# Chunked attention with a gated feed-forward network on one core: tighter attention buffers and an earlier end of the weight sums

## The chip, the cores and the metric

The kernel runs on one core of a Trainium2 chip. The metric is the device time of one execution in microseconds; a kernel's time is the median of its runs. The kernel before takes 924.37 us (three runs, 924.31 to 925.99).

## The reference, cut to what matters

```
def _attn_ref(q, k, v):                      # (8, 8, 576, 64) each
    q_c = q.reshape(B, H, 9, 64, 64)         # and k_c, v_c: chunks of 64 tokens
    scores = scale * np.matmul(q_c, k_c.transpose(0, 1, 2, 4, 3))
    scores = scores - np.max(scores, axis=-1, keepdims=True)
    attn = np.exp(scores)
    attn = attn / (np.sum(attn, axis=-1, keepdims=True) + 1e-09)
    return np.matmul(attn, v_c)
...
    x = attn_out.transpose(0, 2, 1, 3).reshape(4608, 512)
    gate = 1.0 / (1.0 + np.exp(-(x @ w_gate)))       # 512 x 1536
    return gate * (x @ w_val) @ w_out                # 1536 x 512
```

Everything is fp32. The kernel writes a number as the sum of two parts that TensorE multiplies at its faster rate ("high", rounded, and "low", what is left) and makes three products of them, so one fp32 matmul is three instructions.

## The kernel before

The 4608 tokens are nine blocks of 512. Blocks 0 to 2 are computed directly, blocks 3 to 8 in three pairs by Strassen's scheme, with 7 products instead of 8 for each 2x2 block product.

**Direct blocks.** A step handles one of twelve groups of 128 hidden units for one block: `hidden` (L315) runs 24 matmuls of 512 columns for gate and value (L313), a sigmoid on ScalarE (L322), the product on VectorE (L324) and the split into high and low part `hx` (ScalarE L327, VectorE L328). `down` then runs 12 matmuls (L339) on the step before's hidden values. After the twelfth group `evacuate` copies the four finished tiles from PSUM, by VectorE (L357) and ScalarE (L355) in turn, into the two buffers of the tag "ob" (the last two tiles of block 2 into one of their own), from where they are stored.

**Attention** runs ahead of the blocks, as a generator `flow` in which each `yield` is a place to wait: `tick` gives it credit and lets it go on, `insert` places the matmuls. It goes by pairs of units (a unit is 256 tokens of four heads). For a pair: `products2` makes the scores (64 matmuls of 64x64, L192), VectorE takes off the maximum (L721, L722), ScalarE exponentiates (L726), VectorE sums, inverts, multiplies (L744 to L749) and transposes 32x32 blocks in place (L753); then 16 copies bring the blocks to their transposed places (`pbd`): all on ScalarE (L766) during blocks 1 and 2, half of them on GpSimd (L764) in the Strassen part (`joined`). `values2` multiplies with the values (64 matmuls, L207), and the result becomes the input block (`xt`, or `raw` for the Strassen part). Keys lie in `kbd` and transposed blocks in `pbd` with zeros beside each 64x64 block, since the first units (another routine) multiply blocks of twice the width; a unit's keys come with two loads. The scores after the maximum lie in one buffer `pr`.

**Weight sums.** The Strassen part needs sums and differences of weight blocks, which are made while blocks 1 and 2 run and put in DRAM. That is 36 items (`keep`, `keep_sums`): 24 of the sort stored in `sums`, 12 for the output weights, stored in `stream`. An item is two or three additions on VectorE (L400; L404 and L407) into a tile `a_val`, then five instructions on GpSimd: three additions (L409 to L411), a copy that makes the high part `a_high` (L413) and a subtraction that leaves the low part in `a_val` (L414). Two or four stores on SP's queue follow (L417; L421), high part first. `a_val` comes from the two buffers of "ob", which the block outputs use too. In `rest` 32 items are handed out evenly over the steps, 1.5 a step,

```
keep(min(32, 3 * (x + part) // 4))
```

so that the last falls in the step before the last of block 2; the four others (`late`, tile `a_late`, all on GpSimd) follow in groups 2, 4, 5 and 7 of the first Strassen pair.

**Operands.** Before the Strassen part starts, VectorE takes differences of the `raw` blocks (`differ` L461, `operands` L477), ScalarE makes high parts `xc` (L481) and VectorE low parts (L489). These stand among the last steps of block 2.

**Strassen part.** For each pair and each of twelve weight groups `first`, `middle` and `last` run 42 matmuls of products into `cx`, `cy`, `cz` (L499), with the sums that join them on VectorE, ScalarE and GpSimd (GpSimd: L527, L583, L584), and `outward` the output products (L640). `load_group` fetches the weights: L438 those that are given, L441 the sums.

The order on TensorE, VectorE and ScalarE is the order of the program (`manual_schedule`). On GpSimd and on SP, which issues all loads and stores, a scheduler sets it. An engine or queue takes its instructions in order, so one that waits holds all behind it.

## Time and profile before

| what | value |
|---|---|
| runs | 924.31, 924.37, 925.99 us |
| the profiled execution | 921.2 us |
| its span in the profile | 919.4 us |
| mean granted TensorE clock | 0.987 |
| TensorE busy | 891.3 us, 97% |
| VectorE, ScalarE, GpSimd busy | 607.5, 429.1, 268.3 us |

The profile is of one execution, whose own time is 921.2 us; the 1.8 us that it has over the span lie around the recorded instructions. Busy time counts instructions and not the waits of an engine. The granted clock is the share of TensorE's full speed. Times in the rows are microseconds from the start of the span. "[1.80 <-DVE ob L357]" means that the engine sat idle for 1.80 us before, until VectorE's instruction of line 357 that writes `ob` released it. PE is TensorE, DVE VectorE, ACT ScalarE, POOL GpSimd.

### The profile page before, as it was taken

Reading aid. Unit: us, or ns where it says so; the run is one execution under the profiler, and the core shown is the slowest. Engines: PE = TensorE matmul, PEld = TensorE weight load, DVE = VectorE, ACT = ScalarE, POOL = GpSimd, SP = SyncE. Lnnn points to the kernel's source line nnn. Section 1 sums busy time; section 2 is a strip of 40 time slices with the busy share of each in tenths; the row PEclk is TensorE's granted clock in tenths of the full one; section 3 lists DMA queues with packets and bytes.
Section 4 is the critical chain, followed back from the end, with each engine's and each line's share of the span. In section 5 each row is a group of like instructions: output and inputs, shape, how many; then the busy total and the mean of one; then the engine's idle time right before and its main releaser. Section 6 shows DMA issues by size and latency. Waiting matters only on the chain. (4 is left out here: it accounts for less than half of the span.)

```text
span 919.4 us, 15150 instructions
## 1 busy us (share of the span) xinstructions
PE 891.3 (97%) x5748; PEld 726.5 (79%) x5748; DVE 607.5 (66%) x894; ACT 429.1 (47%) x768; POOL 268.3 (29%) x325
## 2 busy tenths in 40 slices
PE   6999999999999998898999999999999999999998
PEld 4788879888877886687788888878788888888886
DVE  6999874656655559664666896566678953434884
ACT  5899753455544563254553642455336321112441
POOL 1000000556646658278352000353510002433000
PEclk8999999999999999999999999999999999999999
DMA  8698893344544485566984567775545686554553
GB/s 266 225 312 289 301 324 114 115 139 135 164 155 139 144 232 170 187 221 207 295 305 142 206 222 278 241 244 197 180 149 201 219 277 206 181 206 160 184 206 115
DMA packets 97464, 189.75 MB, mean 206 GB/s; under 512 B 8688, under 2 KB 56304, under 8 KB 93552
## 3 DMA queue, kind: packets, MB, share of 16 engines
q1 hardware_dynamic: 97392, 188.78, 61.6%
q8 instruction: 46, 0.75, 0.3%
q14 instruction: 26, 0.21, 0.1%
HBM read 146.28 MB, written 42.47 MB: 205 GB/s over the span
## 5 line engine op out<-in xcount | busy, mean ns | idle before, releaser
L313 PE MATMUL g<-xt,w 128*128 128x512 f32 (+1 forms) x960 | 210.5, 374 | 6.1 <-ACT hf L322 4.1
L313 PEld LDWEIGHTS g<-xt,w 128*128 128x128 f32 x960 | 168.8, 190 | 41.9 <-ACT hf L322 6.7
L640 PE MATMUL d<-hd,wd 128*128 128x512 f32 x756 | 172.4, 389 | 0.1
L640 PEld LDWEIGHTS d<-hd,wd 128*128 128x128 f32 x756 | 141.7, 188 | 30.3 <-DVE hd L620 0.9
L499 PE MATMUL cy<-xc,wr 128*128 128x512 f32 x648 | 159.8, 390 | 2.0 <-ACT ob L355 0.8
L499 PEld LDWEIGHTS cy<-xc,wr 128*128 128x128 f32 x648 | 121.4, 188 | 28.7 <-ACT ob L355 1.5
L499 PE MATMUL cx<-xc,wr 128*128 128x512 f32 x432 | 113.2, 398 | 2.6 <-DVE ob L357 2.6
L499 PE MATMUL cz<-xc,wr 128*128 128x512 f32 x432 | 111.1, 392 | 0.4 <-issue 0.3
L339 PE MATMUL acc<-w,hx 128*128 128x512 f32 x432 | 107.5, 396 | 2.4 <-DVE ob L357 1.8
L499 PEld LDWEIGHTS cx<-xc,wr 128*128 128x128 f32 x432 | 81.7, 191 | 20.5 <-DVE ob L357 3.1
L339 PEld LDWEIGHTS acc<-w,hx 128*128 128x128 f32 x432 | 80.2, 189 | 20.5 <-DVE ob L357 2.2
L499 PEld LDWEIGHTS cz<-xc,wr 128*128 128x128 f32 x432 | 80.3, 188 | 18.4 <-issue 1.6
L409 POOL TENSOR_TENSOR a_val<-a_val 128x128 f32<-128x128 f32 x32 | 16.9, 527 | 225.7 <-DVE a_val L400 212.8
L527 POOL TENSOR_TENSOR hid<-u,hid 128x512 f32<-128x512 f32 x15 | 19.3, 1290 | 205.4 <-DVE u L556 205.2
L515 ACT COPY s1u<-cx 128x512 f32<-128x512 f32 x36 | 21.2, 588 | 110.9 <-PE cx L499 107.4
L619 ACT CAST hd<-hid 128x1024 fp32r<-128x1024 f32 x48 | 49.9, 1051 | 49.2 <-PE d L640 37.3
L766 ACT COPY pbd<-pr 32x256 f32<-32x256 f32 x160 | 64.6, 403 | 5.8 <-DVE pr L753 3.7
L620 DVE TENSOR_TENSOR hd<-hid,hd 128x1024 fp32r<-128x1024 f32 x48 | 58.5, 1223 | 12.4 <-ACT hd L619 12.2
L324 DVE TENSOR_TENSOR hf<-g,hf 128x512 f32<-128x512 f32 (+1 forms) x40 | 25.3, 632 | 58.0 <-ACT hf L322 39.8
L764 POOL COPY pbd<-pr 32x256 f32<-32x256 f32 x64 | 25.3, 395 | 106.6 <-DVE pr L753 86.8
L517 DVE TENSOR_TENSOR s1u<-cy,s1u 128x512 f32<-128x512 f32 x36 | 24.8, 689 | 40.8 <-PE cy L499 40.7
L327 ACT CAST hx<-hf 128x512 fp32r<-128x512 f32 (+1 forms) x40 | 23.1, 578 | 60.9 <-DVE hf L324 60.9
(130 smaller groups left out, 1154.0 us busy)
## 6 DMA issues: line engine op xcount, KB each, us to landing
wr<-sums SPq DMA_DIRECT2D x72, 512.0 KB, 4.8
wd<-stream SPq DMA_DIRECT2D x30, 1024.0 KB, 4.6
w_raw<-w_in SPq DMA_DIRECT2D x36, 512.0 KB, 5.3
wr<-given SPq DMA_DIRECT2D x36, 512.0 KB, 3.8
qt<-q_in SPq DMA_DIRECT2D x36, 256.0 KB, 3.8
kbd<-k_in SPq DMA_DIRECT2D x72, 128.0 KB, 3.9
vt<-v_in SPq DMA_DIRECT2D x36, 256.0 KB, 3.8
given<-w SPq DMA_DIRECT2D x36, 256.0 KB, 4.8
```

The costliest lines, as they stand in the source:

```text
L313: nc.tensor.matmul(ps[:, tok], lhsT=wt[f, which][:, wpart, c:c + P], rhs=x[:, part, i, tok], start=n == 0, stop=n == 11)
L324: nc.vector.tensor_tensor(out=hf, in0=pv, in1=hf, op=ALU.mult)
L327: nc.scalar.copy(hh[:, tok], hf)
L339: nc.tensor.matmul(acc[m, t], lhsT=hx[:, ts], rhs=wt[f, 2][:, wpart], start=f == 0 and i == 0, stop=f == NF - 1 and i == 2,)
L499: nc.tensor.matmul(bank, lhsT=lhs(wpart, c), rhs=x[:, part, c], start=start and k == 0, stop=stop and k == 5, skip_group_check=True)
L515: nc.scalar.copy(s1, x)
L517: nc.vector.tensor_tensor(out=u2, in0=y, in1=s1, op=ALU.add)
L619: nc.scalar.copy(t[:, 0], at)
L620: nc.vector.tensor_tensor(out=t[:, 1], in0=at, in1=t[:, 0].bitcast(F32), op=ALU.subtract)
L640: nc.tensor.matmul(bank, lhsT=w[:, o:o + P], rhs=x[:, part], start=p == 0 and opening and i == 0, stop=p == 5 and i == 2, skip_group_check ...
L764: nc.gpsimd.tensor_copy(pb[dst, :, c, h, i, :], ps[src, h::2, k, :])
L766: nc.scalar.copy(pb[dst, :, c, h, i, :], ps[src, h::2, k, :])
```

## The change

- Keys and transposed blocks have no zeros from unit 8 on: a pair's keys are one tile `kt`, with one load a unit instead of two, its transposed blocks one tile `pt`. The four tiles of `kbd` and `pbd` go to a pool of their own with four places (k0, k1, p0, p1), which later tiles take over.
- The room is used twice: every second pair's `pr` lies in place k0 instead of the old buffer, and `a_val` becomes a tile for two items that alternates between place p1 and "spare", so four items are held instead of two. `a_high` takes the two buffers of "ob" instead.
- Sums are handed out at 1.8 a step instead of 1.5. The four late ones follow in groups 1, 3, 5 and 7.
- The 16 copies of a pair are half ScalarE's and half GpSimd's in blocks 1 and 2 too, in one piece. ScalarE's copies go from 160 to 112, GpSimd's from 64 to 112.
- The values' matmuls may be placed one tick sooner (`insert(upto, 1)`), the exponential waits for the next tick in blocks 1 and 2.

The numbers of instructions on TensorE and VectorE stay the same.

```diff
--- before.py
+++ after.py
@@ -70,9 +70,9 @@
     zeros = early[:, 0, 0].bitcast(mybir.dt.bfloat16)
     nc.vector.memset(zeros, 0.0)
 
-    kbd = [const.tile([P, 2, 2, 256], F32, name=f"kbd{i}") for i in range(2)]
-    pbd2 = const.tile([P, 2, 8, 2, D], F32, name="pbd")
-    pbd = [pbd2[:, i] for i in range(2)]
+    kp = ctx.enter_context(tc.tile_pool(name="kp", bufs=1))
+    kbd = [kp.tile([P, 2, 2, 256], F32, tag=f"k{i}", name=f"kbd{i}") for i in range(2)]
+    pbd = [kp.tile([P, 8, 2, D], F32, tag=f"p{i}", name=f"pbd{i}") for i in range(2)]
     for i in range(2):
         eng = nc.gpsimd if i else nc.vector
         eng.memset(kbd[i][0:D, :, 1, :], 0.0)
@@ -140,18 +140,24 @@
 
 
     units = [(m, h, u) for m in range(NB) for h in range(2) for u in range(2)]
-    state, both = {}, {}
+    state, both, keys, turned = {}, {}, {}, {}
     xt, raw = {}, {}
 
     def load(j):
         m, h, u = units[j]
         g = 2 * m + h
         qt = ap2.tile([P, 2, 256], F32, name="qt")
-        kb = kbd[j % 2]
         nc.sync.dma_start(qt, q[g, u].rearrange("p (a n) -> p a n", a=2))
-        for i in range(2):
-            s = slice(i * D, (i + 1) * D)
-            nc.sync.dma_start(kb[s, :, i, :], k[g, u, s].rearrange("p (a n) -> p a n", a=2))
+        if j < 8:
+            kb = kbd[j % 2]
+            for i in range(2):
+                s = slice(i * D, (i + 1) * D)
+                nc.sync.dma_start(kb[s, :, i, :], k[g, u, s].rearrange("p (a n) -> p a n", a=2))
+        else:
+            if j // 2 not in keys:
+                keys[j // 2] = kp.tile([P, 2, 2, 256], F32, tag="k1", name="kt")
+            kb = keys[j // 2][:, u]
+            nc.sync.dma_start(kb, k[g, u].rearrange("p (a n) -> p a n", a=2))
         state[j] = dict(qt=qt, kb=kb)
 
     def load_values(j):
@@ -192,14 +198,14 @@
                             nc.tensor.matmul(
                                 sc[i][c * D:(c + 1) * D, at:at + D],
                                 lhsT=s["qt"][i * D:(i + 1) * D, a, n0:n0 + D],
-                                rhs=s["kb"][i * D:(i + 1) * D, a, i, n0:n0 + D], start=True, stop=True)
+                                rhs=s["kb"][i * D:(i + 1) * D, a, n0:n0 + D], start=True, stop=True)
         return [x.rearrange("p (g k) -> p g k", k=D) for x in sc]
 
     def values2(j):
         av = [ps_a.tile([P, 512], F32, tag="psa", name="av") for _ in range(2)]
         for u in range(2):
             s = state.pop(j + u)
-            pb = pbd[(j + u) % 2]
+            pb = turned[j // 2][:, u]
             for c in range(4):
                 at = (4 * u + c) * D
                 for a in range(2):
@@ -207,7 +213,7 @@
                         nc.tensor.matmul(
                             av[i][a * D:(a + 1) * D, at:at + D],
                             lhsT=s["vt"][i * D:(i + 1) * D, a, c, :],
-                            rhs=pb[i * D:(i + 1) * D, 4 * a + c, i, :], start=True, stop=True)
+                            rhs=pb[i * D:(i + 1) * D, 4 * a + c], start=True, stop=True)
         m, h, _ = units[j]
         at = slice(h * 256, (h + 1) * 256)
         if m < FIRST_PAIR and h == 0:
@@ -365,7 +371,7 @@
 
 
 
-    given, sums, highs = {}, {}, {}
+    given, sums, vals = {}, {}, {}
     stream = dp.tile([P, 7, 6, 512], F32, name="stream")
 
     def keep_given(p, which):
@@ -389,8 +395,9 @@
             val, high = place_[:, 0, 0].bitcast(F32).rearrange("p (s n) -> p s n", n=P), place_[:, 1, 0]
         else:
             if c == 0:
-                highs[0] = wp.tile([P, 2, TB], F32R, tag="spare", name="a_high")
-            val, high = mp.tile([P, 4, P], F32, tag="ob", name="a_val"), highs[0][:, c]
+                pool, tag = ((wp, "spare"), (kp, "p1"))[(2 * p + which if which < 2 else p) % 2]
+                vals[0] = pool.tile([P, 2, 4, P], F32, tag=tag, name="a_val")
+            val, high = vals[0][:, c], mp.tile([P, TB], F32R, tag="ob", name="a_high")
         for n in range(2):
             eng = nc.gpsimd if late else nc.vector
             f = 2 * p + n
@@ -714,7 +721,10 @@
                     scv = products2(j, False)
                 if j + 2 < 4 * NB:
                     load(j + 2), load(j + 3)
-                pr = ap2.tile([P, 2, 8, D], F32, name="pr", bufs=1)
+                if j % 4 == 0:
+                    pr = ap2.tile([P, 2, 8, D], F32, name="pr", bufs=1)
+                else:
+                    pr = kp.tile([P, 2, 8, D], F32, tag="k0", name="pr")
                 for i in range(2):
                     yield 1.4
                     mx = sm.tile([P, 8], F32, name="mx")
@@ -753,17 +763,16 @@
                 nc.vector.transpose(out=half, in_=half)
             kept = True
             ps = pr.rearrange("p g (k j) -> p g k j", j=32)
-            pb = pbd2.rearrange("p u (x c) h (i q) -> p (u x) c h i q", c=2, q=32)
+            turned[j // 2] = kp.tile([P, 2, 8, D], F32, tag="p0", name="pt")
+            pb = turned[j // 2].rearrange("p u (x c) (i q) -> p (u x) c i q", c=2, q=32)
             for n in range(16):
-                if n == 0 or n == 8 and not now["joined"]:
+                if n == 0:
                     yield "piece"
                 c, i, h, k = n >> 3, n >> 2 & 1, n >> 1 & 1, n & 1
                 src = slice((2 * c + i) * 32, (2 * c + i + 1) * 32)
                 dst = slice((2 * h + k) * 32, (2 * h + k + 1) * 32)
-                if n % 2 and now["joined"]:
-                    nc.gpsimd.tensor_copy(pb[dst, :, c, h, i, :], ps[src, h::2, k, :])
-                else:
-                    nc.scalar.copy(pb[dst, :, c, h, i, :], ps[src, h::2, k, :])
+                eng = nc.gpsimd.tensor_copy if n % 2 else nc.scalar.copy
+                eng(pb[dst, :, c, i, :], ps[src, h::2, k, :])
 
     ahead = flow()
     now = dict(credit=0.0, ticks=0, since=0, unit=8, early=-1, open=-1, late=-1, up=-1, joined=False, place="")
@@ -785,6 +794,7 @@
                 now["credit"] -= now["item"]
             elif not (now["item"] == "piece" and now["ticks"] > now["since"] and now["place"] != "middle"
                       or now["item"] == "apart" and now["place"] != "middle"
+                      and now["ticks"] > now["since"] - now["joined"]
                       or now["item"] == "wait" and now["ticks"] > now["since"] + (not now["joined"])
                       or now["item"][0] in ("early", "open", "late", "up") and now["item"][1] <= now[now["item"][0]]):
                 break
@@ -861,8 +871,8 @@
                     if part:
                         finish()
                     tick(SHARES[m])
-                    insert(upto, 2)
-                    keep(min(32, 3 * (x + part) // 4))
+                    insert(upto, 1)
+                    keep(min(32, 9 * (x + part) // 10))
                 if m == 2:
                     if f == 8:
                         for which in range(2):
@@ -896,8 +906,8 @@
                     next(ending)
                 if i == 11:
                     now["open"] = n + 1
-                if n == 0 and i in (2, 4, 5, 7):
-                    keep(32 + (2, 4, 5, 7).index(i) + 1, True)
+                if n == 0 and i in (1, 3, 5, 7):
+                    keep(32 + i // 2 + 1, True)
                 if 0 < i < 11:
                     tick(SHARES["middle"], "middle")
             next(ending, None)
```

VectorE, end of block 2, where the Strassen operands are made (`raw`, `xc`; `a_val` are the sums). Before:

```order
L324 TENSOR_TENSOR hf<-g_3604,hf 128x512
L328 TENSOR_TENSOR hx<-hf,hx 128x512
L404 TENSOR_TENSOR a_val<-w 128x256
L407 TENSOR_TENSOR a_val<-w 128x128 x2
L461 TENSOR_TENSOR raw<-raw 128x2x512 x2
L489 TENSOR_TENSOR xc<-raw,xc 128x1024 x3
L324 TENSOR_TENSOR hf<-g_3716,hf 128x512
L328 TENSOR_TENSOR hx<-hf,hx 128x512
L477 TENSOR_TENSOR raw<-raw 128x2x512
L404 TENSOR_TENSOR a_val<-w 128x256
L407 TENSOR_TENSOR a_val<-w 128x128 x2
L489 TENSOR_TENSOR xc<-raw,xc 128x1024 x2
```

With the change:

```order
L330 TENSOR_TENSOR hf<-g_3635,hf 128x512
L334 TENSOR_TENSOR hx<-hf,hx 128x512
L468 TENSOR_TENSOR raw<-raw 128x2x512 x2
L496 TENSOR_TENSOR xc<-raw,xc 128x1024 x3
L484 TENSOR_TENSOR raw<-raw 128x2x512
L330 TENSOR_TENSOR hf<-g_3705,hf 128x512
L334 TENSOR_TENSOR hx<-hf,hx 128x512
L496 TENSOR_TENSOR xc<-raw,xc 128x1024 x2
L484 TENSOR_TENSOR raw<-raw 128x2x512 x2
L330 TENSOR_TENSOR hf<-g_3757,hf 128x512
```

The sums between the differences and the low parts are gone from there; the first row of both fences is the product of the step that makes the differences.

GpSimd, a pair in block 1 or 2: `a_val` and `a_high` are the sums. Before there are sums alone:

```order
L409 TENSOR_TENSOR a_val<-a_val 128x128
L410 TENSOR_TENSOR a_val<-a_val 128x128
L411 TENSOR_TENSOR a_val<-a_val 128x256
L409 TENSOR_TENSOR a_val<-a_val 128x128
L413 CAST a_high<-a_val 128x512
L410 TENSOR_TENSOR a_val<-a_val 128x128
L414 TENSOR_TENSOR a_val<-a_val,a_high 128x512
L411 TENSOR_TENSOR a_val<-a_val 128x256
L413 CAST a_high<-a_val 128x512
```

With the change a pair's eight copies (`pt<-pr`) come between them:

```order
L775 COPY pt<-pr 32x8x32 x4
L416 TENSOR_TENSOR a_val<-a_val 128x128
L775 COPY pt<-pr 32x8x32
L417 TENSOR_TENSOR a_val<-a_val 128x128
L775 COPY pt<-pr 32x8x32
L418 TENSOR_TENSOR a_val<-a_val 128x256
L775 COPY pt<-pr 32x8x32
L420 CAST a_high<-a_val 128x512
L775 COPY pt<-pr 32x8x32
L421 TENSOR_TENSOR a_val<-a_val,a_high 128x512
```

Four copies stand ahead of an item, the others alternate with its instructions.

GpSimd, first Strassen pair, ahead of the second group of copies. Before (the third late item, then a product of the hidden values and the copies):

```order
L404 TENSOR_TENSOR a_late<-w 128x256
L407 TENSOR_TENSOR a_late<-w 128x128 x2
L409 TENSOR_TENSOR a_late<-a_late 128x128
L410 TENSOR_TENSOR a_late<-a_late 128x128
L411 TENSOR_TENSOR a_late<-a_late 128x256
L413 CAST a_late<-a_late 128x512
L414 TENSOR_TENSOR a_late<-a_late 128x512
L527 TENSOR_TENSOR hid<-u_4224,hid 128x512
L764 COPY pbd<-pr 32x8x32 x8
```

With the change (the fourth late item):

```order
L411 TENSOR_TENSOR a_late<-w 128x256
L414 TENSOR_TENSOR a_late<-w 128x128 x2
L416 TENSOR_TENSOR a_late<-a_late 128x128
L417 TENSOR_TENSOR a_late<-a_late 128x128
L418 TENSOR_TENSOR a_late<-a_late 128x256
L420 CAST a_late<-a_late 128x512
L421 TENSOR_TENSOR a_late<-a_late 128x512
L534 TENSOR_TENSOR hid<-u_4226,hid 128x512
L775 COPY pt<-pr 32x8x32 x8
```

The rows have the same kinds and order; the late item is another one.

## Rows read from the trace of the kernel before

**Rows 1.** the page's part 1: engine, busy us (share of the span), instructions

```profile
PE 891.3 (97%) x5748; PEld 726.5 (79%) x5748; DVE 607.5 (66%) x894; ACT 429.1 (47%) x768; POOL 268.3 (29%) x325
```

**Rows 2.** windows: length, busy us of PE, PEld, DVE, ACT, POOL; clock, DMA share, GB/s

```profile
160.00:255.00 95.00, 95.00 (x828) 77.63 (x827) 56.19 (x93) 48.99 (x89) 57.16 (x75) 1.00 0.43 135
255.00:280.00 25.00, 22.57 (x150) 17.78 (x149) 13.18 (x21) 11.59 (x27) 11.08 (x15) 0.93 0.51 163
...
345.00:380.00 35.00, 27.94 (x105) 21.03 (x104) 26.29 (x29) 10.38 (x14) 22.34 (x17) 0.90 0.59 183
...
410.00:446.00 36.00, 32.85 (x310) 25.92 (x308) 19.79 (x31) 15.39 (x31) 28.62 (x40) 0.95 0.74 245
```

**Rows 3.** timeline of TensorE, a steady step: start us, duration us, operation, count

```profile
287.50 5.60 PE L313 MATMUL g<-xt,w 128*128 128x512 f32 x24
...
295.75 1.16 PE L192 MATMUL sc<-kbd,qt 64*64 64x64 f32 x64
```

**Rows 4.** timeline of TensorE, end of block 1; in brackets the idle time before

```profile
261.28 1.52 PE L339 MATMUL acc<-w,hx 128*128 128x512 f32 x6
...
268.80 5.74 PE L313 MATMUL g<-xt,w 128*128 128x512 f32 x24
...
277.88 5.73 PE L313 MATMUL g<-xt,w 128*128 128x512 f32 x24 [0.62 <-ACT hf L322]
```

**Rows 5.** timeline of VectorE, then of ScalarE, end of block 1

```profile
263.86 0.69 DVE L357 COPY ob<-acc 128x512 f32<-128x512 f32 x1 [5.50 <-DMA sums<-a_val]
...
270.58 6.63 ACT L766 COPY pbd<-pr 32x256 f32<-32x256 f32 x16
```

**Rows 6.** timeline of TensorE, end of block 2

```profile
347.52 2.88 PE L339 MATMUL acc<-w,hx 128*128 128x512 f32 x12
353.44 7.34 PE L313 MATMUL g<-xt,w 128*128 128x512 f32 x24 [3.04 <-ACT hf L322]
...
371.42 2.93 PE L499 MATMUL cx<-xc,wr 128*128 128x512 f32 x6 [2.65 <-DVE ob L357]
...
376.60 1.52 PE L499 MATMUL cx<-xc,wr 128*128 128x512 f32 x6
```

**Rows 7.** timeline of VectorE, of ScalarE and of GpSimd, end of block 2

```profile
345.46 1.52 DVE L404 TENSOR_TENSOR a_val<-w 128x256 f32<-128x256 f32 x1 [2.32 <-DMA stream<-a_val]
...
347.30 2.61 DVE L461 TENSOR_TENSOR raw<-raw 128x1024 f32<-128x1024 f32 x2
...
349.95 2.94 ACT L481 CAST xc<-raw 128x1024 fp32r<-128x1024 f32 x3 [5.81 <-DVE raw L461]
...
369.76 2.12 POOL L414 TENSOR_TENSOR a_val<-a_val,a_high 128x512 f32<-128x512 f32 x1
```

**Rows 8.** timeline of TensorE, first Strassen group

```profile
418.72 0.79 PE L207 MATMUL av<-pbd,vt 64*64 64x64 f32 x8 [1.24 <-POOL pbd L764]
...
443.39 1.63 PE L499 MATMUL cy<-xc,wr 128*128 128x512 f32 x6 [0.67 <-DMA wr<-sums]
```

**Rows 9.** timeline of GpSimd, then of SP's queue, first Strassen group

```profile
410.58 0.74 POOL L404 TENSOR_TENSOR a_late<-w 128x256 f32<-128x256 f32 x1 [4.01 <-DMA stream<-a_late]
...
417.41 3.49 POOL L764 COPY pbd<-pr 32x256 f32<-32x256 f32 x8
...
422.50 10.27 SPq L421 DMA_DIRECT2D stream<-a_late  x3
```

**Rows 10.** the tile a_val, GpSimd's instructions: count, duration ns min/median/max, first to last start

```profile
L409 POOL TENSOR_TENSOR a_val<-a_val x32: 450/460/1376, 166.8 to 365.1; 128x128 f32<-128x128 f32 x32
L410 POOL TENSOR_TENSOR a_val<-a_val x32: 453/462/1324, 167.3 to 365.7; 128x128 f32<-128x128 f32 x32
L411 POOL TENSOR_TENSOR a_val<-a_val x32: 725/738/1607, 167.9 to 366.5; 128x256 f32<-128x256 f32 x32
L413 POOL CAST a_high<-a_val x32: 604/611/1493, 168.7 to 368.2; 128x512 fp32r<-128x512 f32 x32
L414 POOL TENSOR_TENSOR a_val<-a_val,a_high x32: 1272/1291/2155, 169.4 to 369.8; 128x512 f32<-128x512 f32 x32
```

## The prediction, made before the run

> **What bounds the kernel now.** I read the page first: TensorE is busy for 891.3 of 919.4 us, the others far less [rows 1]. So time can only be won where TensorE waits, or where its clock was lowered after a wait. The windows say where that is [rows 2]. From 160 to 255 us TensorE is busy all the time at a granted clock of 1.00. It idles for 25.00 - 22.57 = 2.43 us between 255 and 280, for 7.06 us between 345 and 380 and for 3.15 us between 410 and 446, and there the clock is 0.93, 0.90 and 0.95. Counting a window's missing clock share as lost time too (25 x 0.07 + 35 x 0.10 + 36 x 0.05 = 7.1 us), some 19.7 us are lost in these three places. Whatever the change does elsewhere lies beside a TensorE that is full.
>
> The unit for the sums is a steady step: 36 matmuls of 512 columns take 295.75 - 287.50 = 8.25 us, so one takes 0.229 us, and a block of 64 small attention matmuls 1.16 us [rows 3].
>
> Loss A, the end of block 1: from 261.28 to 268.80 run 12 matmuls and one attention block in 7.52 us [rows 4]; 12 x 0.229 + 1.16 = 3.91 would do, so 3.6 are lost, and 0.62 more at 277.88. The other engines tell why [rows 5]: the output copy of VectorE at 263.86 had waited 5.50 us for a store of weight sums (same two buffers "ob"), and the later wait is for a sigmoid behind 16 block copies of ScalarE, 6.63 us long. Loss B, the end of block 2: from 347.52 to 376.60 run 12+24+12+6+12+6+6 = 78 matmuls in 29.08 us; 78 x 0.229 = 17.9, so 11.2 are lost [rows 6]. There VectorE's weight sum at 345.46 waits 2.32 us for its buffer's store, so the differences behind it come late, ScalarE's casts at 349.95 have waited 5.81 us for these, the sigmoid is queued behind the casts, and TensorE waits 3.04 us for the sigmoid. The wait of 2.65 us at 371.42 is for an output copy on the same full VectorE, which still interleaves weight sums; GpSimd's last sum ran at 369.76 [rows 7]. Loss C, the first Strassen group: values matmuls wait 1.24 us for GpSimd's copies at 417.41, queued behind a late sum that waited 4.01 us for a store at 410.58; and 0.67 at 443.39 is for weights whose load came late: SP's queue had stood for 10.27 us from 422.50 at a late sum's stores [rows 8, 9].
>
> **The change part by part.** *Early sums.* Now 32 items at 1.8 a step need 32/1.8 = 17.8 steps instead of 21.3, and the order shows none left in the last four steps of block 2, where before five were interleaved with the differences and lower halves. So the VectorE wait of 2.32 us, the sums between the differences and the GpSimd work of loss B go, and with them its waits and the half clock after them. Is something else late next? In the first of those steps VectorE has two differences (2.61 us for the two while it shared the time with sums [rows 7]) and then lower halves; it can run over a step of 8.25 us by a little and has three lighter steps to recover, and TensorE needs the hidden values only a step later. I take all of it: **-11.2**. Bounds: nothing (a new chain as long as the old) to 11.2.
>
> *Sums in four-deep buffers apart from "ob".* The output copies no longer share buffers with the sums' low part. They share them with the high part now, which is made and stored ahead of the low one. Of A's 3.6 + 0.6 = 4.2 us I take **-3.7**: ScalarE's 16 copies become 8, so the sigmoid comes about 3.3 us sooner and the 0.62 goes whole; of the 3.6 I leave 0.5 for a wait on the new neighbour. Bounds: 0.6 to 4.2.
>
> *GpSimd.* It has to do more in less time. An item is five instructions. Between 160 and 255 us 75 took 57.16 us, so 57.16 / 15 = 3.81 an item [rows 2]; the medians make 3.56, the slowest of each 7.96 [rows 10]. Per step: 1.8 x 3.81 = 6.86, and for each of six pairs eight copies of 3.49 us together [rows 9], 6 x 3.49 / 17.8 = 1.18; 8.04 in all. A step is 8.25 plus twelve attention blocks over 17.8 steps, 12 x 1.16 / 17.8 = 0.78, that is 9.03. GpSimd is 89% full: it keeps up, and I cost it **0** while its cover, the 1.0 us left a step, holds. It falls behind from an item of (9.03 - 1.18) / 1.8 = 4.36 us on.
>
> *Keys, transposed blocks, values a tick sooner.* One key load instead of two (28 issues fewer on SP), nothing removed on TensorE: **0** where TensorE is full. The values matmuls stand at least a group of 36 matmuls (8.25 us) behind their copies; GpSimd's half takes 3.49 us, with one item of 3.81 mixed in 7.30. Cover left: 1.0 us.
>
> *Late sums.* In the new orders all four stand ahead of the copies of 417.41, and the last stores ahead of the loads in question, so the wait at 443.39 goes: **-0.9** (0.67, and some lower clock; at least 0). The wait at 418.72 stays: where the third late item stood before the copies, the fourth now does, and it still needs an earlier item's store; with fewer loads on SP that store may come a little sooner. I take **-0.5**, between -4.3 (the window's 3.15 + 1.8, less 0.67) and, with an item's medians of 3.56 more in front of the copies, +3.6.
>
> Sum: 11.2 + 3.7 + 0.9 + 0.5 = 16.3 us less. The profiled execution took 921.2 us, with 1.8 around the span; 921.2 - 16.3 = 904.9. The median of the three runs, 924.37, is 3.2 above the profiled one, so I predict 904.9 + 3.2 = **908.1 us** for the median.
>
> **Rivals.** *GpSimd falls behind (slower).* For: it goes from 57.16 / 95 = 60% to 89% busy, and where VectorE runs two-operand work beside it, as after 345 us, an item cost up to 7.96. Against: between 160 and 255 us it ran beside the same VectorE work at 3.81. The buffers let it trail by two items more; from then on VectorE waits and the delay is TensorE's. If every second item paid the full price, one would be (3.56 + 7.96) / 2 = 5.76, a step 10.37 + 1.18 = 11.55, the lag 17.8 x (11.55 - 9.03) = 44.9, less 2 x 5.76, that is 33.4 us: 908.1 + 33.4 = 941.5. It turns slower where 17.8 x (1.8 t + 1.18 - 9.03) - 2 t passes 16.3, at an item t of 5.2 us. If every third item paid it, t = 3.56 + 4.40 / 3 = 5.03, the lag 17.8 x 1.20 = 21.4, less 10.1, is 11.3: 919.4. The rows bear this on: a 128x128 sum takes 0.46 us, and 1.32 at its slowest [rows 10]. The Trainium skill ("SBUF — State Buffer", section "Who interferes with whom") says that a VectorE instruction with two operands in SBUF and a GpSimd instruction that reads SBUF exclude each other, and the later one blocks for the whole of the other. By that rule, which speaks against copies on GpSimd and sums packed closer, the sum would be nearer the 919.4 of this rival than my 908.1; the trace agrees that such blocking happens (0.46 to 1.32), but at 3.81 against 3.56 an item it was rare in the steady steps, hence the small chance below.
>
> *A stays.* The output copy waits for the high part's store as it did for the low part's, or copies that now share GpSimd with sums reach the values matmuls after their 1.0 us of cover. Then 3.7 of the gain goes: 911.8.
>
> *B moves.* The differences and casts alone keep the sigmoid late, as at 353.44, with the half clock after it: 3.04 idle plus g's 7.34 - 5.60 = 1.74 us come back: 912.9 [rows 3, 6].
>
> *C goes too.* The fourth late item gets its buffer early enough: 908.1 - 3.8 = 904.3.
>
> *The change does not do what it says.* The order shows the moved sums, so only the timing can undo it.
>
> **How the numbers follow.** The forecast 0.59; A stays 0.13, B moves 0.09, every third item slow 0.06, C goes too 0.05; GpSimd far behind 0.05; several losses together up to about no change 0.03. The range takes in the first five and a microsecond below 904: 903 to 920. A measurement of this kernel tells 0.2% (about 1.8 us) from no change. Faster by more than that: 0.90; within: 0.03; slower: 0.07 (GpSimd far behind, 0.05, and a mishap that I have not named, 0.02).
>
> **What would show it.** Right: TensorE without idle time from 255 to 380 us but for under 1 us at the end of block 1; no weight sums after about 320 us until the Strassen group; GpSimd some 89% busy between 165 and 320 with items near 3.8 us; the wait for GpSimd's copies still there, near 400 us. Wrong: GpSimd items over 4.4 us and VectorE waiting for stores of sums in block 2; a sigmoid wait at the end of block 2; TensorE waiting for "pt".

## The result and the profile after

The changed kernel takes 913.66 us (median of four runs, 910.0 to 916.83) against 924.34 for the kernel before, measured beside it; the ratio is 0.9889, with a 95% interval of 0.9841 to 0.9936. A second set of runs, below, gave 0.9913 (0.9889 to 0.9938). So it is faster by about 1%, some 10 us; 16.3 were forecast. The profiled execution went from 921.2 to 913.41 us, its span from 919.4 to 911.6.

The windows of the changed kernel, the same stretches and columns as [rows 2]:

```profile
160.00:255.00 95.00, 95.00 (x828) 77.52 (x827) 67.47 (x100) 40.82 (x70) 77.02 (x109) 1.00 0.45 145
255.00:280.00 25.00, 22.53 (x201) 17.45 (x203) 15.10 (x23) 6.40 (x15) 15.28 (x24) 0.93 0.51 175
...
345.00:380.00 35.00, 34.54 (x153) 28.28 (x152) 21.65 (x28) 10.62 (x16) 6.41 (x9) 1.00 0.64 209
...
410.00:446.00 36.00, 32.50 (x364) 26.32 (x365) 16.15 (x25) 14.25 (x28) 18.65 (x25) 0.91 0.73 246
```

TensorE's idle time between 345 and 380 us is 35.00 - 34.54 = 0.46 us instead of 7.06, at full clock. Between 255 and 280 it is as before, 2.47, and from 410 to 446 larger, 3.50 instead of 3.15 at a clock of 0.91. One of the three losses went, and two stayed.

Windows cut at fixed times mix what happened with when. A table by places in the program says more: five stretches of TensorE, from one instruction to the same instruction in every kernel. **Start** ends with the first matmul of the second step of block 2, the step in which most of block 1's outputs are copied out; **outputs** is that one step; **steps** are the eight after it, to the first matmul of the eleventh step of block 2; **operands** ends at the fifth Strassen product; **first pair** is eight weight groups; **rest** runs to the end. Microseconds, each the difference of two start times in the timeline of TensorE:

| kernel | start | outputs | steps | operands | first pair | rest | span |
|---|---|---|---|---|---|---|---|
| before | 255.8 | 13.0 | 73.3 | 35.9 | 92.4 | 449.0 | 919.4 |
| changed | 256.7 | 13.2 | 74.2 | 25.2 | 94.3 | 448.0 | 911.6 |
| changed, again | 259.6 | 13.4 | 74.0 | 25.3 | 94.8 | 449.9 | 916.9 |
| e1_pace | 256.3 | 9.5 | 73.5 | 38.0 | 94.4 | 450.3 | 922.1 |
| e7_beforepace | 257.2 | 14.1 | 76.4 | 24.5 | 91.6 | 449.0 | 912.8 |
| e5_copies | 263.6 | 9.5 | 81.3 | 24.5 | 94.1 | 448.5 | 921.4 |
| e2_hold | 256.4 | 9.5 | 81.0 | 24.5 | 93.8 | 448.0 | 913.2 |
| e3_late | 258.4 | 13.4 | 74.0 | 26.1 | 88.2 | 448.1 | 908.2 |
| e4_both | 254.7 | 9.5 | 79.7 | 25.9 | 88.2 | 448.5 | 906.5 |
| e8_high | 259.3 | 10.7 | 75.8 | 26.2 | 95.6 | 449.3 | 917.0 |
| e9_highlate | 258.4 | 10.8 | 75.6 | 27.0 | 88.7 | 448.2 | 908.8 |
| e11_head | 254.3 | 15.4 | 77.0 | 24.5 | 88.2 | 448.2 | 907.5 |
| e10_pace30 | 252.5 | 10.0 | 73.7 | 27.1 | 88.1 | 448.2 | 899.7 |

(What the expectations call "the ten steps", 87.4 us with the change, are "outputs" and "steps" together, nine steps in fact; their "tenth step of block 2" is the eleventh, and their "fifth cx product" the fifth product of any kind. The expectation of e1_pace ends "operands" one product, 1.36 us, sooner.) Of the change's 7.8 us, operands give -10.7, start +0.9, outputs +0.2, steps +0.9, first pair +1.9 and rest -1.0.

**The end of block 2.** TensorE's timeline, where [rows 6] had 29.08 us from 347.52 to 376.60:

```profile
349.51 2.88 PE L345 MATMUL acc<-w,hx 128*128 128x512 f32 x12
352.86 5.74 PE L319 MATMUL g<-xt,w 128*128 128x512 f32 x24 [0.46 <-ACT hf L328]
...
367.95 1.52 PE L506 MATMUL cx<-xc,wr 128*128 128x512 f32 x6
```

The same instructions take 367.95 - 349.51 = 18.44 us, with one wait of 0.46 us for the sigmoid.

**The end of block 1.** TensorE, VectorE, ScalarE, GpSimd and SP's queue, to be held against [rows 4, 5]:

```profile
265.74 0.96 PE L345 MATMUL acc<-w,hx 128*128 128x512 f32 x3 [1.43 <-ACT ob L361]
267.74 2.37 PE L345 MATMUL acc<-w,hx 128*128 128x512 f32 x6 [1.04 <-DVE ob L363]
269.91 6.60 PE L319 MATMUL g<-xt,w 128*128 128x512 f32 x24
...
261.31 0.69 DVE L363 COPY ob<-acc 128x512 f32<-128x512 f32 x1 [4.02 <-DMA sums<-a_high]
267.00 0.69 DVE L363 COPY ob<-acc 128x512 f32<-128x512 f32 x1 [4.99 <-DMA out<-ob]
...
265.10 0.59 ACT L361 COPY ob<-acc 128x512 f32<-128x512 f32 x1 [9.72 <-DMA sums<-a_high]
267.85 0.59 ACT L361 COPY ob<-acc 128x512 f32<-128x512 f32 x1 [2.16 <-DMA out<-ob]
...
261.77 0.61 POOL L420 CAST a_high<-a_val 128x512 fp32r<-128x512 f32 x1
...
262.41 0.53 SPq L424 DMA_DIRECT2D sums<-a_high  x1
...
264.37 4.42 SPq L364 DMA_DIRECT2D out<-ob  x4
```

The high part of the last sum, which now has one of the two buffers of "ob", is made at 261.77, and its store is issued at 262.41. ScalarE's output copy at 265.10 had waited 9.72 us for it. The outputs' own stores follow on SP behind it, at 264.37, and the next two copies wait for these. TensorE waits 1.43 and 1.04 us, then runs the 24 matmuls at 269.91 slowly: 6.60 us against a steady 5.60; the granted clock from 268 to 272 us was 0.57. GpSimd's instructions stand back to back up to that high part: it was late.

**The first Strassen pair**, against [rows 8, 9]:

```profile
405.95 2.88 PE L506 MATMUL cy<-xc,wr 128*128 128x512 f32 x12
412.65 0.94 PE L213 MATMUL av<-pt,vt 64*64 64x64 f32 x8 [3.82 <-POOL pt L775]
414.44 2.22 PE L213 MATMUL av<-pt,vt 64*64 64x64 f32 x56 [0.84 <-POOL pt L775]
416.59 2.63 PE L506 MATMUL cx<-xc,wr 128*128 128x512 f32 x6
...
404.55 0.74 POOL L411 TENSOR_TENSOR a_late<-w 128x256 f32<-128x256 f32 x1 [6.62 <-DMA stream<-a_late]
...
411.34 3.50 POOL L775 COPY pt<-pr 32x256 f32<-32x256 f32 x8
...
397.80 2.79 SPq L428 DMA_DIRECT2D stream<-a_late  x4
400.69 0.47 SPq L445 DMA_DIRECT2D wr<-given  x1
401.53 0.33 SPq L448 DMA_DIRECT2D wr<-sums  x1
402.29 1.74 SPq L428 DMA_DIRECT2D stream<-a_late  x2
```

The fourth late item waits 6.62 us for an earlier item's store; before, the third waited 4.01. That store is issued in pieces, and loads of weights stand between them (400.69, 401.53). Counted from the fifth Strassen product, the copies at 411.34 start 42.0 us later, 39.5 before, and TensorE waits 3.82 + 0.84 us where it waited 1.24 + 0.98. The wait at 443.39 is gone, as forecast.

### The profile page after: what moved, and what is told of

The parts are those of the page before. It is cut to its first block, busy times and chain, and to the rows that moved or that the text cites. A ratio compares the mean times of both kernels' runs of the same rounds, so it can differ in the third digit from the quotient of the medians.

```text
span 911.6 us, 15114 instructions
## 1 busy us (share of the span) xinstructions
PE 887.9 (97%) x5748; PEld 725.9 (80%) x5748; DVE 622.3 (68%) x894; ACT 410.0 (45%) x720; POOL 291.7 (32%) x373
## 5 line engine op out<-in xcount | busy, mean ns | idle before, releaser
L506 PEld LDWEIGHTS cy<-xc,wr 128*128 128x128 f32 x648 | 121.5, 188 | 26.1 <-DVE s1u L524 0.8
L775 POOL COPY pt<-pr 32x256 f32<-32x256 f32 x112 | 46.9, 419 | 121.4 <-DVE pr L763 115.6
L775 ACT COPY pt<-pr 32x256 f32<-32x256 f32 x112 | 45.2, 403 | 22.9 <-DVE pr L763 21.4
L563 DVE TENSOR_TENSOR hid<-cz,u 128x512 f32<-128x512 f32 x18 | 12.4, 692 | 56.8 <-PE cz L506 56.7
```

Of the source, the lines that this page charges most:

```text
L506: nc.tensor.matmul(bank, lhsT=lhs(wpart, c), rhs=x[:, part, c], start=start and k == 0, stop=stop and k == 5, skip_group_check=True)
L775: eng(pb[dst, :, c, i, :], ps[src, h::2, k, :])
```

## The experiments

**Is the gain the end of the sums?** e1_pace hands them out as before and leaves all else changed:

```
-                    keep(min(32, 9 * (x + part) // 10))
+                    keep(min(32, 3 * (x + part) // 4))
```

> The changed kernel with the sums handed out at 1.5 a step again (the last five fall among the operands); buffers, copies and the rest as in the change. Theory (the gain is the end of the sums before the operands): the stretch from the tenth step of block 2 to the fifth cx product, 23.9 us with the change and 34.5 before, goes back to 31 to 35 us, and the time rises by 7 to 11 us over the changed kernel, to about 922. Rival (the gain is the deeper buffers, which end the wait for stores): the stretch stays within 2 us of 23.9 and the time near 913.5.

922.09 us, ratio to before 0.9996 (0.9976 to 1.0017): the whole gain is lost. Operands rise from 25.2 to 38.0 us, more than forecast (36.6 as the expectation counts). Its timeline of TensorE:

```profile
360.99 0.73 PE L345 MATMUL acc<-w,hx 128*128 128x512 f32 x2 [2.33 <-ACT hx L333]
...
370.47 2.93 PE L506 MATMUL cx<-xc,wr 128*128 128x512 f32 x6 [4.25 <-DVE ob L363]
```

But outputs fall to 9.5 us, from 13.0 before and 13.2 with the change, although a_high shares "ob" here too. So that sharing alone is not the cause of the loss there.

e7_beforepace is the reverse, the kernel before with this one line of the change:

> The kernel before with the faster handing out of the sums alone (1.8 a step); buffers, copies and values as before. Theory (the end of the sums before the operands is the gain, and the room only makes the faster rate possible): the stretch from the tenth step of block 2 to the fifth cx product falls from 35.9 to 25 to 28 us, but with two buffers for the sums, shared with the outputs, the ten steps before lose part of it, 2 to 8 us more than before's 86.2; the time lies between 912 and 920. Rival (the faster rate needs the room, or VectorE stalls in every step): the ten steps take over 97 us and the time is no better than before, 921 or more.

One execution, 914.63 us, span 912.8: the one line brings nearly all that the whole change brings. Operands fall to 24.5; outputs and steps cost 4.2 us more than before. The room, the copies on GpSimd and the other parts win 3.1 of these back (90.5 to 87.4) and lose 2.7 in the first pair.

**The end of block 1.** e2_hold gives no sums in the three places ahead of the output copies and hands them out after:

```
+ keep({20: 17, 21: 17, 22: 17, 23: 18, 24: 20}.get(x + part, min(32, 9 * (x + part) // 10)))
```

> The changed kernel without sums in the three places ahead of the output copies at the end of block 1; they follow in the next three places. Theory (the output copies waited for the stores of a_high, with which they now share the two buffers of ob): the waits of 4.02 us on VectorE and 9.72 us on ScalarE for those stores go, the idle time of 1.43 + 1.04 us on TensorE at 265 us too, and the time falls by 3 to 4.5 us, to about 910. Rival (the copies wait for the store of the first two output tiles itself, behind other work in SP's queue): the TensorE idle time stays at 1.5 to 2.5 us and the time within 1.5 us of the changed kernel.

Half right. Outputs fall to 9.5 us and the wait for a_high is gone. But the time is 915.7, ratio 0.9938 (0.9919 to 0.9957), not better than the change: the steps take 81.0 us instead of 74.2. VectorE and TensorE there:

```profile
276.93 3.32 DVE L407 TENSOR_TENSOR a_val<-w 128x256 f32<-128x256 f32 x4 [2.74 <-DMA sums<-a_val]
...
284.60 3.20 DVE L407 TENSOR_TENSOR a_val<-w 128x256 f32<-128x256 f32 x4 [1.97 <-DMA sums<-a_val]
...
280.90 3.02 PE L319 MATMUL g<-xt,w 128*128 128x512 f32 x12 [2.32 <-DVE hf L330]
...
298.38 5.73 PE L319 MATMUL g<-xt,w 128*128 128x512 f32 x24 [2.27 <-ACT hf L328]
```

The held sums come close together, VectorE waits for the four buffers, and the sigmoid chain behind it is late. Holding them saved 3.7 us in the outputs and cost 6.8 in the steps.

e5_copies takes the other load off GpSimd:

```
-                eng = nc.gpsimd.tensor_copy if n % 2 else nc.scalar.copy
+                eng = nc.gpsimd.tensor_copy if n % 2 and now["joined"] else nc.scalar.copy
```

> The changed kernel with all 16 copies of a pair on ScalarE again in blocks 1 and 2. Theory (GpSimd, some 87% busy between 166 and 255 us, is behind, and that makes the output copies wait for the last a_high): GpSimd has 48 copies fewer, its busy share there falls under 80%, the step at the end of block 1, 13.2 us with the change and 9.3 to 9.5 without loss, shortens by 2 us or more, and TensorE's wait for pt at 305 us goes. Rival (the shared buffers make the wait whatever GpSimd's load): the step stays within 1 us of 13.2. Against both, the sigmoid queues behind 6.6 us of copies again, for up to 0.6 us a pair.

Outputs fall to 9.5, and GpSimd's share between 166 and 255 us from 77.02 / 89 = 87% to 60.90 / 89 = 68%. But the sigmoid stands behind ScalarE's 16 copies, and TensorE waits 1.95, 3.72 and 4.50 us for it, where 0.6 was forecast:

```profile
194.37 5.78 PE L319 MATMUL g<-xt,w 128*128 128x512 f32 x24 [1.95 <-ACT hf L328]
...
244.50 7.06 PE L319 MATMUL g<-xt,w 128*128 128x512 f32 x24 [3.72 <-ACT hf L328]
...
307.02 8.19 PE L319 MATMUL g<-xt,w 128*128 128x512 f32 x24 [4.50 <-ACT hf L328]
```

```profile
237.20 6.63 ACT L775 COPY pt<-pr 32x256 f32<-32x256 f32 x16 [5.97 <-DVE pr L763]
```

One execution, 923.5 us. The copies themselves start late here: ScalarE had waited 5.38, 5.97 and 6.97 us for VectorE's transposes, for which it did not wait before ([rows 5], 270.58). With half of the copies on GpSimd the changed kernel had no wait for the sigmoid above 0.46 us between 160 and 380 us. As TensorE stalled for 3.72 us just ahead of the outputs, GpSimd had that time to catch up, so this run alone does not prove the lag.

e8_high gives a_high a place of its own, for the second buffer of `pr`:

```
+                vals[1] = kp.tile([P, 2, TB], F32R, tag="k0", name="a_high")
-            val, high = vals[0][:, c], mp.tile([P, TB], F32R, tag="ob", name="a_high")
+            val, high = vals[0][:, c], vals[1][:, c]
```

> The changed kernel with a_high as a pair tile in place k0, so that ob holds block outputs alone; the second buffer of pr is given up for it. Theory (sharing ob is the loss at the end of block 1): no wait for stores of a_high by VectorE's and ScalarE's output copies, the step there 9.3 to 10 us instead of 13.2, and the time 3 to 4.5 us under the changed kernel. Rival (the second buffer of pr is what lets the differences come early, or its loss costs as much): VectorE or GpSimd wait for pr or for k0's stores in the steps of blocks 1 and 2, and the ten steps, 87.4 us, get no shorter than 86.

918.47 us, ratio 0.9936 (0.9906 to 0.9967). No output copy waits for a_high any more, and outputs take 10.7 us, 2.5 less than with the change but above the forecast 9.3 to 10; the steps cost 1.6 more, so that the two together take 86.5, as the rival said. The time is a miss: the output copies still wait for each other's stores, and with one `pr` the values matmuls wait 1.07 and 0.45 us for VectorE's subtraction into it, a wait that the changed kernel does not have.

e11_head raises the rate ahead of the output copies by a head start and lowers it later (with the edit of e3_late, below):

```
+                    keep(min(32, 2 + 6 * (x + part) // 7))
```

> e3_late with the 32 early items at 1.71 a step after a start two items higher, ending at the same place. Theory (lag of GpSimd): busy 85% instead of 89%, the step at the end of block 1 shortens from 13.4 to 11 to 13 us; the time 907 to 910. Rival (it is the place of the last item ahead of the output copies alone): no change from e3_late's 87.4 us in the ten steps.

Neither the theory nor the rival came: outputs grow to 15.4 us, steps to 77.0; 913.09 us, ratio 0.9888 (0.9863 to 0.9913). The head start keeps GpSimd 83.03 / 89 = 93% busy up to the outputs, and the order has two sums in a row on VectorE just ahead of them. e10_pace30 lowers the rate: 30 early items at 1.6 a step, and six late ones in buffers of their own.

```
+                    keep(min(30, 2 + 4 * (x + part) // 5))
...
+                if n == 0 and i in (0, 1, 4, 6):
+                    keep({0: 33, 1: 34, 4: 35, 6: 36}[i], True)
```

> The changed kernel with 30 early items at 1.6 a step (two of them ahead of the others at the start) and six late ones, of which the first four stand at the head of the first Strassen pair and none needs the store of a late item shortly before it. Theory (what is left of the loss in blocks 1 and 2 is GpSimd's lag, which a rate nearer 1.5 ends): the ten steps of blocks 1 and 2 take 83 to 85 us instead of 87.4, the stretch behind them 24.5 to 26.5, the Strassen stretch 88 to 89 as in e3_late; the time 902 to 906. Rival (late items beside the differences block VectorE as the sums did before): the stretch from the tenth step to the fifth cx product goes back over 28 us and the time is no better than e3_late's 910.5.

906.16 us (901.48 to 909.96), ratio 0.9828 (0.98 to 0.9855): the lowest of all, just above the forecast, though its interval overlaps that of e9_highlate below. Outputs take 10.0 and steps 73.7, 83.7 together. GpSimd is as busy as ever before it (81.21 / 89 = 91% from 166 to 255), but where the outputs come it waits for VectorE instead of running late. GpSimd, then VectorE's first output copy, in e10_pace30, and in e11_head:

```profile
253.07 0.46 POOL L423 TENSOR_TENSOR a_val<-a_val 128x128 f32<-128x128 f32 x1 [0.69 <-DVE a_val L414]
...
254.96 0.61 POOL L427 CAST a_high<-a_val 128x512 fp32r<-128x512 f32 x1
...
253.47 0.69 DVE L363 COPY ob<-acc 128x512 f32<-128x512 f32 x1 [0.47 <-DMA sums<-a_high]
```

```profile
255.23 0.46 POOL L424 TENSOR_TENSOR a_val<-a_val 128x128 f32<-128x128 f32 x1
...
258.68 0.61 POOL L428 CAST a_high<-a_val 128x512 fp32r<-128x512 f32 x1
...
258.81 0.69 DVE L363 COPY ob<-acc 128x512 f32<-128x512 f32 x1 [5.21 <-DMA sums<-a_high]
```

The same high part in e1_pace, and in e5_copies:

```profile
258.25 0.61 POOL L420 CAST a_high<-a_val 128x512 fp32r<-128x512 f32 x1
```

```profile
264.92 0.61 POOL L420 CAST a_high<-a_val 128x512 fp32r<-128x512 f32 x1
```

In e10_pace30 the last high part is made at 254.96, 2.4 us after the step's start (252.5), in e1_pace 1.9 after it and in e5_copies 1.3; in e11_head at 258.68, 4.4 after (254.3), and in the changed kernel 5.1. The three early ones have outputs of 10.0, 9.5 and 9.5 us, the two late ones 15.4 and 13.2. The place of the last sums is not the cause: by their formulas the changed kernel, e10_pace30, e1_pace and e5_copies hand out the last four items ahead of the output copies at the same four places, and all but e1_pace (16) have handed out 19 by then; what differs is how far GpSimd is behind. So GpSimd's lag at that moment, through the buffers of "ob", is the loss, not its mean share. It does not set the size alone: e11_head, which has handed out 20 items, loses more than the changed kernel with a smaller lag. Operands rise to 27.1, above the forecast 24.5 to 26.5: a product waits 1.82 us for weights at 355.10, in a stretch into which GpSimd and SP have taken late sums.

**The first pair.** In e3_late the third late item lies in place p1 and the fourth in the two buffers of "ob":

```
+            if len(kept) < 2:
+                if kept:
+                    pair = kp.tile([P, 2, TB], F32R, tag="p1", name="a_late")
+                    val, high = pair[:, 0], pair[:, 1]
+                else:
+                    val, high = [mp.tile([P, TB], F32R, tag="ob", name="a_late") for _ in range(2)]
```

> The changed kernel with the third late item in place p1 and the fourth in the two buffers of ob, so that neither needs the store of an earlier late item. Theory (the wait of 6.62 us of the fourth item for that store holds the copies behind it): GpSimd has no such wait, TensorE's 3.82 + 0.84 us for the copies near 412 us go or fall below 1.5, the clock stays full there, and the time falls by 5 to 8 us, to about 907. Rival (the copies are late by the amount of work on GpSimd ahead of them): TensorE still waits 3 us or more for them there and the time stays within 2 us of 913.5.

910.53 us, ratio 0.988 (0.9856 to 0.9903); the first pair takes 88.2 us instead of 94.3, TensorE has no idle time from 380 to 446 us and the clock is full. In the whole time the gain is smaller than the forecast 5 to 8 us, and the ratio's interval overlaps both of the changed kernel's, so it is read from the stretch:

```profile
380.00:410.00 30.00, 30.00 (x250) 24.54 (x250) 19.30 (x30) 15.88 (x31) 15.74 (x26) 1.00 0.76 254
410.00:446.00 36.00, 36.00 (x394) 29.21 (x393) 21.75 (x34) 19.75 (x35) 18.38 (x24) 1.00 0.74 248
```

The edit did more than take away the wait. The late items now start at 347.8, 359.1, 390.5 and 439.3 us, the last behind the copies, where with the change they start at 356.2, 387.9, 389.4 and 404.6, all ahead of them. So GpSimd has less work there too, as the rival would have it. That the wait alone would do is argued from its size: 6.62 us, more than the 3.82 + 0.84 that TensorE lost.

e4_both joins e2_hold and e3_late:

> The edits of the two runs before together. If the two losses are independent the gains add: 8 to 12 us less than the changed kernel, 902 to 906. If removing one uncovers another wait behind it (GpSimd 89% full with the held sums, or SP's queue), less than 6 us.

911.93 us, ratio 0.9889 (0.9859 to 0.992): no better than e3_late, since the held sums cost in the steps more than they save at the outputs (89.2 us together, 87.4 in e3_late). e9_highlate joins e8_high and e3_late:

> The edit of the run before with that of e3_late (the late items without a common store). If both losses go without a new wait: 8 to 11 us under the changed kernel, 903 to 906. If the second buffer of pr was needed: as e3_late, 909 to 912.

909.1 us, ratio 0.9833 (0.9802 to 0.9863): at the lower end of the second forecast. Its stretches are those of the two runs: 86.4 us for outputs and steps, 88.7 for the first pair.

The changed kernel was run once more beside e10_pace30:

> The changed kernel once more, for a second look at its stretches and its ratio to the kernel before beside the two runs above: 0.985 to 0.993; the ten steps 87 to 88 us, the stretch behind 24.5 to 26, the Strassen stretch 93.5 to 95.

914.47 us; all stretches as expected but the start, 2.9 us longer for the same instructions.

## Why the prediction was right or wrong

The direction was right and the measured 913.66 us lies in the range, but 908.1 was 5.6 us too low. Against the profiled execution the sum was -16.3, and -7.8 came. Of the 8.5 us between them, 4.8 are the end of block 1 with the steps behind it, 3.3 the first pair and 0.5 the operands; start and rest cancel to 0.1. The range held because it was drawn around rivals as dear as this, "A stays" (911.8) among them; of the terms of the sum only the early sums and the 0.9 came.

- **Early sums, -11.2: right.** Operands gave -10.7, the wait for the sigmoid fell from 3.04 to 0.46 us, and e1_pace and e7_beforepace (one execution) show that the rate alone makes it, in either kernel.
- **Outputs of block 1, -3.7: wrong.** The stretch grew by 0.2. The step that failed is "of the 3.6 I leave 0.5 for a wait on the new neighbour". The rival that the copies wait for the high part's store as they did for the low part's, at 0.13, is what happened, with GpSimd's lag as the reason that it was so long. The 0.62 for the sigmoid at 277.88 did go, but a wait for it of 0.30 at 298.49 and one for GpSimd's copies of 0.32 at 304.93 are new; these and the slow matmuls at 269.91, 1.0 us over a steady step, lie in the steps, which grew by 0.9.
- **GpSimd keeps up, 0: wrong in kind.** The share was right, 87% against 89%, and the items stayed near their price: the medians of an item's five instructions make 3.59 us, 3.56 before. But a mean share says nothing of where GpSimd stands at one moment: a cover of 1.0 us a step does not take up a pair's copies of 3.5 us at once, and at the outputs GpSimd was about 3 us later than in e1_pace or e10_pace30.
- **Late sums, -0.9 and -0.5: the first right, the second wrong in sign.** The step that failed is "with fewer loads on SP that store may come a little sooner": the scheduler put loads of weights between the pieces of the store, the wait for it grew from 4.01 to 6.62 us, and the first pair grew by 1.9 us. The whole loss there, 94.3 - 88.2 = 6.1 us, goes in e3_late, with buffers that need no such store and fewer late items ahead of the copies.
- The start (+0.9) and the rest (-1.0) say nothing of the change: the same kernel run again took 2.9 and 1.9 us more there.
- Of the signs named for being wrong, TensorE's wait for "pt" in block 2 (0.32 us) and a sigmoid wait at the end of block 2 (0.46) came, both small. In [rows 10] the slowest 128x128 sum is 1.38 us, not 1.32; nothing hangs on it.

The rule of the Trainium skill that the prediction weighed ("SBUF — State Buffer", section "Who interferes with whom") fits the traces, but on an engine that I had not priced. Not GpSimd's items but VectorE's additions grew. The tile a_val's row of them before, and then that of the change with GpSimd's first sum:

```profile
L400 DVE TENSOR_TENSOR a_val<-w x48: 382/419/1524, 165.9 to 310.7; 128x256 f32<-128x256 f32 x48
```

```profile
L407 DVE TENSOR_TENSOR a_val<-w x48: 381/676/1519, 166.7 to 285.5; 128x256 f32<-128x256 f32 x48
L416 POOL TENSOR_TENSOR a_val<-a_val x32: 450/466/910, 167.6 to 335.8; 128x128 f32<-128x128 f32 x32
```

The median went from 419 to 676 ns, GpSimd's from 460 to 466; VectorE was busy for 67.47 us instead of 56.19 from 160 to 255 us with 100 instructions instead of 93. As VectorE had 29% idle there, it cost TensorE nothing that the timeline shows. The same row from 160 to 260 us in e5_copies, and in e1_pace:

```profile
L407 DVE TENSOR_TENSOR a_val<-w x36: 382/418/1518, 166.0 to 255.9; 128x256 f32<-128x256 f32 x36
```

```profile
L407 DVE TENSOR_TENSOR a_val<-w x32: 382/612/1517, 166.4 to 255.9; 128x256 f32<-128x256 f32 x32
```

With the sums at 1.8 a step but the copies on ScalarE the median stays at 418 ns, and at 1.5 a step with half of the copies on GpSimd it is 612. So the growth came with GpSimd's copies and not with the closer sums; which instruction held which no run takes apart.

## What to carry to other kernels

A buffer that two engines' results share joins their lateness: before moving work to another engine, ask where that engine stands when the shared buffer is next needed, not how full it is on average. A change of many parts is best split by one-line versions in both directions: here the rate of handing out work alone gave nearly all of the gain, and the parts around it moved the waits. Compare executions by stretches from instruction to instruction, as the whole time can hide a gain of 6 us, like that of e3_late, behind differences in other stretches.

## What the runs showed that was not expected

Up to the outputs of block 1 the changed kernel took 256.7 us in one profile and 259.6 in another; the difference is larger than some of the effects. Part of such a difference is there early, before the variants differ in what they run: a group of ten gate matmuls starts at 25.39 us in e10_pace30 and at 27.99 in the changed kernel, and 16 score matmuls shortly before took 1.09 and 1.97 us.

```profile
20.70 1.09 PE L179 MATMUL sc<-kbd,qt 128*64 128x128 f32 x16
...
25.39 1.45 PE L319 MATMUL g<-xt,w 128*128 128x256 f32 x10 [0.22 <-DVE xt L308]
```

```profile
20.93 1.97 PE L179 MATMUL sc<-kbd,qt 128*64 128x128 f32 x16
...
27.99 1.45 PE L319 MATMUL g<-xt,w 128*128 128x256 f32 x10 [0.22 <-DVE xt L308]
```

The granted clock of the first 26 us was 0.87 in e10_pace30, 0.74 in the changed kernel and 0.95 in its second profile, which took the longest of the three. So the clock alone does not explain the spread, and what does was not tried.
